# Turning the query maxima of a linear attention kernel: a transpose of 128 stationary columns in place of a product with 18

## The chip, the cores and the metric

The kernel runs on one core of a Trainium2 chip. The metric is the device time of one execution in microseconds (us). Three runs of the kernel before took 1091.09 to 1091.14 us, with a median of 1091.14.

## The reference, cut to what matters

A linear attention over 4 batches and 8 heads, 576 tokens of 64 numbers each, is followed by two feed-forward blocks. All inputs are float32.

```python
def phi(x):                                  # for q and for k
    proj = einsum('bhsd,df->bhsf', x, w_phi)            # 64 -> 128 features
    proj = proj - max(abs(proj), axis=-1)               # one maximum per token and head
    return concatenate([exp(proj), exp(-proj)], axis=-1)
kv, z = einsum('bhsf,bhsd->bhfd', phi(k), v), sum(phi(k), over s)
x = (phi(q) @ kv) / (phi(q) . z + 1e-6)                 # (2304, 512) in all
h = x @ moe_w_in;   x = maximum(0.01 * h, h) @ moe_w_out             # 512 -> 2048 -> 512
g = x @ moe2_w_gate
out = (g * sigmoid(g) * (x @ moe2_w_val)) @ moe2_w_out               # 512 -> 1536 -> 512
```

The change touches the line with the maximum, for the queries alone.

## The kernel before, in words

**Precision.** Most large products are made of parts: a float32 operand is split into a high and a low part of TensorE's float32r type (a copy on ScalarE and a subtraction on VectorE), and three products high*high, high*low and low*high are summed in PSUM. These are the rows with 128 x 288 outputs: a half of a batch, 288 tokens, is one PSUM bank. A plain float32 product takes two passes in the hardware, so it has two LDWEIGHTS and two MATMUL in the trace; a float32 transpose (`k_tr`, line 240) has one of each.

**Stages.** Attention of batch 0 comes first, alone. After that the feed-forward layers of batch b run as a list of "units" (`u_l1`, `u_gate`, `u_val`, `u_out`; the matmuls of line 615, for batch 3 and one block of batch 2 those of line 741), and the attention of batch b + 1 is spread between them: its keys beside the first block, its queries beside the second. So the queries of batches 1, 2 and 3 stand at about 187 to 340, 465 to 600 and 740 to 850 us of the span. The last batch has only feed-forward layers beside it.

**Queries.** For batches 1 to 3 the work of a batch is 8 groups: 4 pairs of heads (j), each in two halves of 288 tokens (t). For one group:

- `q_p` projects with features on the partitions (lines 336 and 337, two heads, one PSUM bank of 288 columns each), turns blocks of 32 x 32 on VectorE (338) and takes maxima (340). What is left is `m`, tile `mqt`: 128 partitions x 18. Partition 32 g + i, column (head, k) holds the maximum over the 32 features of block g for token 32 k + i.
- `q_m_t` turns `m` on TensorE, so that the 4 feature blocks lie in one partition: a matmul with `m` as the stationary operand (18 columns) and the identity as the moving one (line 346). The result goes into unused columns 288 to 415 of the group's second PSUM bank, partitions 0 to 17. VectorE then takes the maximum over the 4 blocks (348), splits it (351, 59) and lays it out as `mrow` with a 0/1 mask (356).
- `q_exp` adds minus the maximum to the projections by a matmul (367) and ScalarE makes the two exponentials (375, 376). `q_num` multiplies with the keys' sums (393), `q_fin` divides (401 to 411) and writes `xh` and `xl`, which the first layer reads.

In batch 1 the numerator (393) is a plain float32 product, in batches 2 and 3 it is made of float32r parts.

**Constants.** `cst_sb` is one SBUF tile of 128 partitions: the identity `ident` (128 columns), then `mask` (18) and `mask_t` (9). It is loaded once. `k_tr` reads `ident` as well.

**Order.** The program is written out as calls; the Tile framework then orders each engine's instructions by priorities and by a simulated time line (`schedule_with_timeline_sim=True`). The engines run their lists in order, and wait for each other by semaphores that the framework sets from the tiles' regions. All loads are issued on SyncE. So a changed cost of one instruction can change the order of others.

Of the kernel before, what the change touches and what calls it, by code (L numbers as in the profile page):

```python
# [7 lines left out]
F32 = mybir.dt.float32  # L8
# [9 lines left out]
P = 128  # L18
# [9 lines left out]
HT = S // 2  # L28

NB = HT // 32  # L30

NC = P + 18 + NB

OFF = (0, 128, 256, 352, 448)
VAL = (128, 128, 96, 96, 128)
# [6 lines left out]
def linear_attention_two_mlps(ctx: ExitStack, tc, qT, kT, vt, w_phi, w1, w2, wg, wv, w3, cst, out):  # L42
    nc = tc.nc
    act, dve, pe, pool = nc.scalar, nc.vector, nc.tensor, nc.gpsimd
# [9 lines left out]
    def T(shape, dt, tag, bufs, pool=sb):  # L54
        uid[0] += 1
        return pool.tile(shape, dt, tag=tag, name=f"{tag}_{uid[0]}", bufs=bufs)

    def sub(o, a, b):
        dve.tensor_tensor(out=o, in0=a, in1=b, op=ALU.subtract)  # L59
# [3 lines left out]


    cst_sb = const.tile([P, NC], F32, name="cst_sb")
    ident = cst_sb[:, 0:P]
    mask = cst_sb[:, P : P + 18]
    mask_t = cst_sb[:, P + 18 : NC]
    sel = const.tile([P, 4, P], F32R, name="sel")
    ones = const.tile([P, P], F32R, name="ones")  # L70
    wst_h = const.tile([P, F], F32R, name="wst_h")
# [6 lines left out]
    def constants():  # L78
        signs = T([P, 4, P], F32, "es", 5)
        nc.sync.dma_start(out=cst_sb, in_=cst[:, 0:NC])  # L80
        nc.sync.dma_start(out=signs.rearrange("p h f -> p (h f)"), in_=cst[:, NC:])
        zero = T([P, F], F32, "es", 5)
# [12 lines left out]
    def bk(b=1):  # L95

        if b == 0:
            return T([P, 512], F32, "pm", 4, psm)
        return T([P, 512], F32, "pa", 4, psa)
# [186 lines left out]
    qs, pt, mq, mrow, qfh, qfl, qn, dn = ({} for _ in range(8))  # L286
# [41 lines left out]
    def q_p(b, j, t):  # L328

        c = slice(HT * t, HT * t + HT)  # L330
        tp = T([P, 2, NB, 32], F32, "pk", 5)
        for h in range(2):
            bank = pt[b, j, h, t] = bk(b)
            ps = bank[:, 0:HT]
            a = qs[b, j][h][:, c]
            pe.matmul(ps, wst_h, a, start=True, stop=False)
            pe.matmul(ps, wst_l, a, start=False, stop=True)
            dve.transpose(out=tp[:, h].rearrange("p a b -> p (a b)"), in_=ps)
        m = mq[b, j, t] = T([P, 2, NB], F32, "mqt", 2)
        dve.tensor_reduce(out=m, in_=tp, axis=AX.X, op=ALU.max, apply_absolute_value=True)  # L340

    def q_m_t(b, j, t):

        m = mq.pop((b, j, t)).rearrange("p h k -> p (h k)")
        turned = pt[b, j, 1, t][0 : 2 * NB, HT : HT + P]
        pe.matmul(turned, m, ident, start=False, stop=True, skip_group_check=True)  # L346
        top = T([2 * NB, 32], F32, "top", 2)
        dve.tensor_reduce(out=top, in_=turned.rearrange("r (g i) -> r i g", g=4), axis=AX.X, op=ALU.max)
        x = mm[2 + t]
        hi = x[0 : 2 * NB]  # L350
        dve.tensor_copy(hi, top)
        sub(x[32 : 32 + 2 * NB], top, hi.bitcast(F32))
        if t == 0:
            mrow[b, j] = T([P, 2 * NB, 32], F32R, "mrow", 1)
        r = mrow[b, j][:, NB * t : NB * t + NB]
        dve.tensor_tensor(
            out=r,
            in0=x.bitcast(F32).rearrange("p (o i) -> p o i", o=1).to_broadcast([P, NB, 32]),
            in1=mask_t.rearrange("p (k o) -> p k o", o=1).to_broadcast([P, NB, 32]),
            op=ALU.mult,  # L360
        )
# [79 lines left out]
    def q_steps_t(b):  # L441


        groups = [(j, t) for j in range(NP) for t in range(2)]
        n = len(groups)
        steps = []
        for i in range(n + 2):
            one, two = [], []
            if i >= 2:
                j, t = groups[i - 2]  # L450
                one.append(lambda j=j, t=t: q_num(b, j, 0, t))
                two.append(lambda j=j, t=t: (q_num(b, j, 1, t), q_fin(b, j, t)))
            if 1 <= i <= n:
                j, t = groups[i - 1]
                one.append(lambda j=j, t=t: q_exp(b, j, 0, t))
                two.append(lambda j=j, t=t: q_exp(b, j, 1, t))
            if i < n:
                j, t = groups[i]
                if t == 0:
                    one.append(lambda j=j: q_split(b, j))  # L460
                one.append(lambda j=j, t=t: q_p(b, j, t))
                two.append(lambda j=j, t=t: q_m_t(b, j, t))
                if t == 1 and j + 1 < NP:
                    two.append(lambda j=j: load_q(b, j + 1))
                if t == 1 and j + 1 == NP and b + 1 < B:
                    two.append(lambda: load_k(b + 1, 0))
            steps += [one, two]
        return steps
# [586 lines left out]
    pre, made, start = 8, 0, 30  # L1055
# [26 lines left out]
def _constants():  # L1082
    import numpy as np

    c = np.zeros((P, NC + 4 * P), np.float32)
    c[:, 0:P] = np.eye(P)
    signs = c[:, NC:].reshape(P, 4, P)
    blocks = [(s, a) for s in range(NST) for a in range(VAL[s] // 32)]
    for p in range(P):
        a, r = divmod(p, 32)  # L1090
        if r >= 4 * NST:
            continue
        st, h = divmod(r % (2 * NST), 2)
        signs[p, h] = -1.0
        for k, (s2, a2) in enumerate(blocks):
            c[p, P + k] = float(s2 == st and a2 == a)
    for part in (0, 32):
        for h in range(2):
            for k in range(NB):
                c[part + NB * h + k, P + 18 + k] = 1.0  # L1100
                signs[part + NB * h + k, 2 + h] = -1.0
    return c

# [47 lines left out]
```

## Time and profile before

| | |
|---|---|
| three runs, median (lowest to highest) | 1091.14 us (1091.09 to 1091.14) |
| the profiled execution: its span, first to last instruction | 1092.6 us |
| TensorE matmul busy in it | 1062.8 us, 97% |
| VectorE, ScalarE, GpSimd busy | 808.8, 656.2, 21.8 us |
| mean granted TensorE clock | 0.997 of 2.4 GHz |
| line 346, matmuls (24 calls, two passes each) | x48, 9.4 us of busy time |

The page shows no time around the span of the profiled execution; that span is 1.5 us longer than the median of the timed runs. Busy time of TensorE is the union of matmuls that overlap in a pipeline: a 128 x 288 matmul is shown with 298 ns, but one starts every 0.13 us. What an instruction costs TensorE is therefore read from the distance of starts, not from its duration.

### The profile page before, as it was taken

The numbers are of one execution on the slowest core, as the hardware profiler recorded it, in microseconds if no ns is written. First come the engines' busy times: TensorE is split into PE (matmuls) and PEld (weight loads), VectorE is DVE, ScalarE is ACT, GpSimd is POOL, SyncE is SP. The second block draws the span as 40 slices with busy tenths as digits, with TensorE's granted clock in tenths as the row PEclk, the third lists the DMA queues.
The fourth block names the chain that finished last, engine by engine and source line by source line (L and its number), as shares of the span: only waits on it lengthen the run. The fifth ranks groups of instructions, "written<-read, shape, count | busy, mean of one in ns | idle before, by whom it ended". The sixth has DMA issues, their size and how long they took to land.

```text
span 1092.6 us, 20353 instructions
## 1 busy us (share of the span) xinstructions
PE 1062.8 (97%) x7560; PEld 1023.3 (94%) x7560; DVE 808.8 (74%) x1761; ACT 656.2 (60%) x1467; POOL 21.8 (2%) x56
## 2 busy tenths in 40 slices
PE   7889999999999999999999988999999999999998
PEld 6668999989899999999999988999999999999998
DVE  6897797888899888779676864857779742458473
ACT  7878886768777787546553575644542334426441
POOL 1000100000000000000000000000000000000000
PEclk9999999999999999999999998999999999999999
DMA  9736767555666887767454386346978768748652
GB/s 326 235 114 204 240 208 259 172 183 177 210 201 230 335 304 268 263 237 242 164 177 145 111 332 235 126 175 228 313 243 297 287 216 303 275 157 306 216 178 96
DMA packets 98771, 245.61 MB, mean 225 GB/s; under 512 B 19952, under 2 KB 28400, under 8 KB 98672
## 3 DMA queue, kind: packets, MB, share of 16 engines
q1 hardware_dynamic: 94640, 229.62, 60.6%
q0 software_dynamic: 4032, 14.68, 3.4%
q8 instruction: 60, 0.98, 0.4%
q14 instruction: 39, 0.32, 0.1%
HBM read 178.73 MB, written 65.54 MB: 224 GB/s over the span
## 4 chain that ended last, share of the span: by engine, by line
PE 80%; DMA 8%; ACT 6%; DVE 4%; issue 1%; SPq 1%; ACTq 0%; DVEq 0%
PE pm L615 55%; PE pa L741 8%; PE pm L741 4%; PE pa L202 4%; PE pa L393 3%; DMA wi<-in_w_dram 2%; DMA wi<-parts 2%; PE pa L161 2%; DMA wr<-kept 1%; ACT wr L519 1%; DMA sums<-wr 1%; DVE wr L534 1%; PE pm L301 1%; PE pa L346 1%; ACT wi L520 0%
## 5 line engine op out<-in xcount | busy, mean ns | idle before, releaser
L615 PE MATMUL pm<-xh,wi 128*128 128x288 f32 x1664 | 351.7, 298 | 2.4 <-DVE es L656 1.8
L615 PE MATMUL pm<-gp,wo 128*128 128x288 f32 x2256 | 337.5, 297 | 0.8 <-DVE acc L682 0.5
L615 PEld LDWEIGHTS pm<-gp,wo 128*128 128x128 f32 x2256 | 311.1, 188 | 5.2 <-issue 1.9
L615 PEld LDWEIGHTS pm<-xh,wi 128*128 128x128 f32 x1664 | 271.8, 188 | 6.8 <-DVE es L656 2.3
L615 PE MATMUL pm<-xl,wi 128*128 128x288 f32 x832 | 246.7, 297 | 0.0
L615 PEld LDWEIGHTS pm<-xl,wi 128*128 128x128 f32 x832 | 156.3, 188 | 1.4 <-issue 0.6
L682 DVE TENSOR_TENSOR acc<-pm,acc 128x288 f32<-128x288 f32 x160 | 70.5, 450 | 45.2 <-PE pm L615 43.1
L59 DVE TENSOR_TENSOR gp<-es,gp 128x576 fp32r<-128x576 f32 x94 | 70.5, 751 | 29.9 <-ACT gp L62 29.2
L62 ACT ACTIVATE gp<-es 128x576 fp32r<-128x576 f32 x94 | 64.3, 688 | 27.9 <-DVE es L663 22.8
L741 PE MATMUL pm<-xh,wi 128*128 128x288 f32 x304 | 71.6, 303 | 6.0 <-DMA wi<-parts 5.2
L59 DVE TENSOR_TENSOR wi<-wr,wi 128x512 fp32r<-128x512 f32 x96 | 64.8, 682 | 13.2 <-ACT wi L544 12.8
L544 ACT ACTIVATE wi<-wr 128x512 fp32r<-128x512 f32 x96 | 59.5, 633 | 13.1 <-PE pm L615 5.2
L741 PEld LDWEIGHTS pm<-xh,wi 128*128 128x128 f32 x304 | 53.2, 193 | 7.8 <-DVE fl L59 3.7
L59 DVE TENSOR_TENSOR fl<-ff,fh 128x512 fp32r<-128x512 f32 (+1 forms) x72 | 50.9, 712 | 11.0 <-ACT fh L62 10.8
L520 ACT ACTIVATE wi<-wi 128x512 int32<-128x512 uint32 x60 | 41.5, 692 | 23.1 <-DMA wi<-in_wv_dram 10.7
L519 ACT ACTIVATE wr<-wi 128x512 f32<-128x512 f32 x60 | 41.2, 690 | 16.4 <-DMA wi<-in_w_dram 8.6
L396 ACT ACTIVATE dn<-pa 64x288 f32<-64x288 f32 x64 | 26.0, 406 | 36.1 <-PE pa L393 35.2
L62 ACT ACTIVATE fh<-ff 128x512 fp32r<-128x512 f32 (+1 forms) x72 | 47.0, 664 | 0.8
L643 ACT ACTIVATE es<-pm 128x288 f32<-128x288 f32 x72 | 28.8, 418 | 29.7 <-PE pm L741 17.1
L741 PE MATMUL pm<-xl,wi 128*128 128x288 f32 x152 | 45.6, 300 | 0.0
L534 DVE TENSOR_TENSOR wr<-wr,wi 128x512 uint16<-128x512 uint16 x60 | 44.9, 751 | 0.8
L202 PE MATMUL pa<-ff,pk 128*128 128x256 f32 (+1 forms) x160 | 42.6, 383 | 2.4 <-issue 1.9
(192 smaller groups left out, 2073.4 us busy)
## 6 DMA issues: line engine op xcount, KB each, us to landing
wi<-parts SPq DMA_DIRECT2D x96, 512.0 KB, 5.9
wo<-parts SPq DMA_DIRECT2D x77, 512.0 KB, 6.6
parts<-wi SPq DMA_DIRECT2D x56, 512.0 KB, 4.6
wi<-in_w_dram SPq DMA_DIRECT2D x44, 512.0 KB, 5.1
wr<-kept SPq DMA_DIRECT2D x72, 256.0 KB, 4.2
parts<-wo POOLq DMA_DIRECT2D x28, 512.0 KB, 5.1
kept<-wr SPq DMA_DIRECT2D x40, 256.0 KB, 4.2
wi<-in_wv_dram SPq DMA_DIRECT2D x12, 512.0 KB, 4.1
```

The lines of the kernel that those rows point to most:

```text
L59: dve.tensor_tensor(out=o, in0=a, in1=b, op=ALU.subtract)
L62: act.activation(o, a, AF.Copy)
L202: pe.matmul(ps[:, 256 * h : 256 * h + 256], v[:n, h].rearrange("p a d -> p (a d)"), part[b, j, s][:n, h].rearrange("p a f -> p (a f)"), st ...
L393: pe.matmul(ps, w, x, start=(i == 0), stop=(i == len(ops) - 1))
L519: act.activation(t, high.bitcast(F32), AF.Abs, scale=REBIAS)
L520: act.activation(low, low.bitcast(U32), AF.Copy, scale=2.0**-29)
L534: dve.tensor_tensor(out=t16, in0=t16, in1=e16, op=ALU.add)
L544: i = act.activation(t[:, 0], r, AF.Copy)
L615: m = pe.matmul(ps, w, x[:, c], start=(i == 0), stop=(i == n - 1))
L643: act.activation(o, i, AF.Prelu, alpha=0.01)
L682: dve.tensor_tensor(out=acc[o][:, t], in0=ps, in1=acc[o][:, t], op=ALU.add)
L741: m = pe.matmul(ps, a, b, start=start and n == 0, stop=stop and n == 5, skip_group_check=True)
```

## The change

The maxima no longer go to a tile of their own. `cst_sb` grows by 36 columns in front of the identity. Two windows of 128 columns, `tops[0]` (columns 0 to 127) and `tops[1]` (18 to 145), begin with the 18 columns that the maxima of half t = 0 or t = 1 are written to. `q_m_t` gives the whole window to TensorE as stationary operand, in transpose mode, and writes 128 x 128 numbers to PSUM, of which partitions 0 to 17 are read as before. What stands in the other columns of a window (the other half's maxima, part of the identity) ends in partitions that nobody reads. The constants' load grows from 155 to 191 columns.

```diff
-NC = P + 18 + NB
+TOPS = 4 * NB
+NC = TOPS + P + 18 + NB
...
-    ident = cst_sb[:, 0:P]
-    mask = cst_sb[:, P : P + 18]
-    mask_t = cst_sb[:, P + 18 : NC]
+    tops = [cst_sb[:, 2 * NB * t : 2 * NB * t + P] for t in range(2)]
+    ident = cst_sb[:, TOPS : TOPS + P]
+    mask = cst_sb[:, TOPS + P : TOPS + P + 18]
+    mask_t = cst_sb[:, TOPS + P + 18 : NC]
...
-        m = mq[b, j, t] = T([P, 2, NB], F32, "mqt", 2)
+        m = tops[t][:, 0 : 2 * NB].rearrange("p (h k) -> p h k", h=2)
         dve.tensor_reduce(out=m, in_=tp, axis=AX.X, op=ALU.max, apply_absolute_value=True)

     def q_m_t(b, j, t):

-        m = mq.pop((b, j, t)).rearrange("p h k -> p (h k)")
-        turned = pt[b, j, 1, t][0 : 2 * NB, HT : HT + P]
-        pe.matmul(turned, m, ident, start=False, stop=True, skip_group_check=True)
+        turned = pt[b, j, 1, t][:, HT : HT + P]
+        pe.matmul(
+            turned, tops[t], ident, is_transpose=True, start=False, stop=True, skip_group_check=True
+        )
+        turned = turned[0 : 2 * NB]
         top = T([2 * NB, 32], F32, "top", 2)
```

The columns of `_constants` move by the same 36.

The order of instructions changes with it, in the stretches of the span in which batches 1 to 3 have their queries. On TensorE the kernel has the same matmuls in both, and 1340 of the 7315 in its list stand at another place, by at most 68 places; between 566 and 709 us of the span before, and from 813 us on, the orders agree.

VectorE, batch 3, first pair of heads, before. The second row is the maximum of half t = 0 (line 340), the sixth that of half t = 1, and the tenth the reduction behind the turn of half t = 0 (348); `pk` is the tile of turned blocks.

```order
L338 STREAM_TRANSPOSE pk_9791<-pa_9796 128x288
L340 TENSOR_REDUCE mqt_9660<-pk_9651 128x18
L682 TENSOR_TENSOR acc_8634<-pm_9611,acc_8634 128x288
L59 TENSOR_TENSOR pk_9960<-raw_9861,pk_9960 64x576
L682 TENSOR_TENSOR acc_8634<-pm_9625,acc_8634 128x288
L340 TENSOR_REDUCE mqt_9800<-pk_9791 128x18
L59 TENSOR_TENSOR pk_9961<-raw_9861,pk_9961 64x576
L682 TENSOR_TENSOR acc_8700<-pm_9662,acc_8700 128x288
L682 TENSOR_TENSOR acc_8700<-pm_9676,acc_8700 128x288
L348 TENSOR_REDUCE top_9697<-pa_9656 18x32
```

The same place now. Lines of the program are 1 to 4 higher in the changed kernel: 338 is 340, 340 is 342, 348 is 352, 59 is 60 and 682 is 686.

```order
L340 STREAM_TRANSPOSE pk_9774<-pa_9779 128x288
L342 TENSOR_REDUCE cst_sb<-pk_9635 128x18
L686 TENSOR_TENSOR acc_8618<-pm_9595,acc_8618 128x288
L60 TENSOR_TENSOR pk_9942<-raw_9843,pk_9942 64x576
L686 TENSOR_TENSOR acc_8618<-pm_9609,acc_8618 128x288
L60 TENSOR_TENSOR pk_9943<-raw_9843,pk_9943 64x576
L686 TENSOR_TENSOR acc_8684<-pm_9645,acc_8684 128x288
L686 TENSOR_TENSOR acc_8684<-pm_9659,acc_8684 128x288
L352 TENSOR_REDUCE top_9680<-pa_9640 18x32
L342 TENSOR_REDUCE cst_sb<-pk_9774 128x18
```

The maximum of half t = 1 stood ahead of the reduction `top` of half t = 0 and now stands behind it. In the other 23 groups it stands behind it in both kernels.

TensorE, batch 1, the turn of the last of the 8 groups, before (line 346; `gp` and `wo` are operands of the second layer, `xh`, `xl` and `wi` of a layer of the block behind it).

```order
L615 MATMUL pm_3893<-gp_3670,wo_3679 128x288 x3
L615 MATMUL pm_3893<-gp_3765,wo_3776 128x288
L615 MATMUL pm_3843<-gp_3765,wo_3776 128x288 x2
L615 MATMUL pm_3857<-gp_3765,wo_3776 128x288 x2
L615 MATMUL pm_3893<-gp_3765,wo_3776 128x288 x2
L346 MATMUL pa_3700<-cst_sb,mqt_3704 18x128
L615 MATMUL pm_3907<-gp_3422,wo_3433 128x288 x3
```

The same turn now (line 347; 619 is the former 615).

```order
L619 MATMUL pm_4027<-xh_2557,wi_3871 128x288
L619 MATMUL pm_4027<-xh_2606,wi_3871 128x288
L619 MATMUL pm_4027<-xl_2607,wi_3871 128x288
L347 MATMUL pa_3693<-cst_sb 128x128
L619 MATMUL pm_4027<-xh_2606,wi_3871 128x288
L619 MATMUL pm_4027<-xh_2651,wi_3871 128x288
L619 MATMUL pm_4027<-xl_2652,wi_3871 128x288
```

It has moved 68 matmuls later, from the output layer into the next unit. The last numerator of this group (393) moved 35 matmuls later, and the first matmul that reads this group's `xh` in the feed-forward layers of batch 1 stands at the same place of the list in both.

## Rows read from the trace of the kernel before

**Rows 1.** The page, its head and the busy time of engines.

```profile
span 1092.6 us, 20353 instructions
...
PE 1062.8 (97%) x7560; PEld 1023.3 (94%) x7560; DVE 808.8 (74%) x1761; ACT 656.2 (60%) x1467; POOL 21.8 (2%) x56
```

**Rows 2.** Stretches: length, busy PE, PEld, DVE, ACT, POOL; clock, DMA share, GB/s.

```profile
187.00:320.00 133.00, 130.20 (x910) 122.34 (x909) 117.19 (x247) 100.55 (x203) 5.84 (x11) 1.00 0.59 194
465.00:600.00 135.00, 135.00 (x1005) 132.00 (x1005) 102.30 (x224) 68.72 (x149) 0.00 (x0) 1.00 0.56 192
740.00:850.00 110.00, 109.39 (x809) 106.06 (x809) 90.94 (x222) 49.68 (x112) 0.00 (x0) 1.00 0.75 261
```

**Rows 3.** Line 346: durations in ns (min/median/max), first and last start.

```profile
L346 PEld LDWEIGHTS pa<-cst_sb,mqt x48: 93/96/98, 191.5 to 840.0; 128*18 128x18 f32 x48
L346 PE MATMUL pa<-cst_sb,mqt x48: 272/278/286, 191.5 to 840.1; 128*18 128x128 f32 x48
```

**Rows 4.** Time line of PE around the first turn: start, length in us, instruction.

```profile
191.15 0.42 PE L615 MATMUL pm<-xh,wi 128*128 128x288 f32 x2
191.50 0.39 PE L346 MATMUL pa<-cst_sb,mqt 128*18 128x128 f32 x2
191.83 0.40 PE L615 MATMUL pm<-xl,wi 128*128 128x288 f32 x1
192.06 0.42 PE L615 MATMUL pm<-xh,wi 128*128 128x288 f32 x2
```

**Rows 5.** Line 240, the transposes of the keys' sums.

```profile
L240 PEld LDWEIGHTS pa<-cst_sb,kvz x64: 138/140/146, 17.7 to 716.7; 128*128 128x128 f32 x64
L240 PE MATMUL pa<-cst_sb,kvz x64: 270/272/328, 17.7 to 716.8; 128*128 128x128 f32 x64
```

**Rows 6.** Time line of PE around single transposes of line 240.

```profile
180.86 0.96 PE L615 MATMUL pm<-gp,wo 128*128 128x288 f32 x6
181.66 0.27 PE L240 MATMUL pa<-cst_sb,kvz 128*128 128x128 f32 x1
181.68 0.38 PE L615 MATMUL pm<-gp,wo 128*128 128x288 f32 x1
181.90 0.27 PE L240 MATMUL pa<-cst_sb,kvz 128*128 128x128 f32 x1
```

**Rows 7.** The chain that ended last: its first and last turn (19 such).

```profile
220.14 0.32 PE pa L346 x2
...
840.00 0.34 PE pa L346 x2
```

**Rows 8.** The chain, longest pieces at 187 to 209, 284 to 309, 762 to 795 us.

```profile
188.70 3.75 DMA wi<-in_wv_dram
...
285.70 5.27 DMA wi<-in_w_dram
...
769.27 7.43 DMA sums<-wr
```

**Rows 9.** What PE waited for, 185 to 325 us: us, times, longest.

```profile
PE pm L615 <- DVE es L656: 1.7, 1, 1.7
```

**Rows 10.** Time line of VectorE, batch 3: maximum t = 1, `top` t = 0.

```profile
743.42 0.74 DVE L340 TENSOR_REDUCE mqt<-pk 128x18 f32<-128x576 f32 x1
...
745.71 0.27 DVE L348 TENSOR_REDUCE top<-pa 18x32 f32<-18x128 f32 x1
```

**Rows 11.** The last numerators (PE) and last results (VectorE, 318 to 345 us) of batch 1.

```profile
328.17 2.10 PE L393 MATMUL pa<-ff,kvh 128*128 128x288 f32 x8
...
L59 DVE TENSOR_TENSOR xl<-xf,xh x3: 444/446/452, 321.7 to 341.2; 128x288 fp32r<-128x288 f32 x3
```

**Rows 12.** PE's longest wait on its time line, and the stretches behind it.

```profile
677.77 0.58 PE L741 MATMUL pm<-xh,wi 128*128 128x288 f32 x1 [3.49 <-DMA wi<-parts]
...
677.00:683.80 6.80, 6.03 (x25) 5.96 (x26) 3.57 (x7) 1.85 (x4) 0.00 (x0) 0.50 0.73 288
684.00:690.00 6.00, 6.00 (x49) 5.96 (x48) 4.57 (x10) 5.15 (x11) 0.00 (x0) 1.00 0.28 89
```

More of the change, by code (lines that the diff above doesn't have):

```diff
@@ L1085, in _constants @@
     c = np.zeros((P, NC + 4 * P), np.float32)
-    c[:, 0:P] = np.eye(P)
+    c[:, TOPS : TOPS + P] = np.eye(P)
     signs = c[:, NC:].reshape(P, 4, P)
@@ L1095, in _constants @@
         for k, (s2, a2) in enumerate(blocks):
-            c[p, P + k] = float(s2 == st and a2 == a)
+            c[p, TOPS + P + k] = float(s2 == st and a2 == a)
     for part in (0, 32):
@@ L1099, in _constants @@
             for k in range(NB):
-                c[part + NB * h + k, P + 18 + k] = 1.0
+                c[part + NB * h + k, TOPS + P + 18 + k] = 1.0
                 signs[part + NB * h + k, 2 + h] = -1.0
```

## The prediction

> **What bounds the kernel now.** I read the page's busy times first, then the stretches in which the queries of batches 1 to 3 stand, then the chain that ended last, and last the time line of TensorE around the instructions in question. TensorE has matmuls running for 1062.8 of 1092.6 us [rows 1]. In the three stretches of the queries that is 130.2 of 133, 135.0 of 135 and 109.4 of 110 us; VectorE, the next busiest, has 117, 102 and 91 [rows 2]. So a slot saved on TensorE there is time saved, as long as nothing else stands just behind it. The chain shows where something does: of the 24 turns 19 lie on it (from the one at 220.14 to the one at 840.00 us [rows 7]), with five of batch 1, all eight of batch 2 and six of batch 3. The five others, at 191.5, 202.9, 290.4, 763.3 and 780.0 us, stand where the chain runs through VectorE, ScalarE and loads, whose longest pieces are the transfers of 3.75, 5.27 and 7.43 us [rows 8].
>
> **The price of a turn before.** A turn is one call and two passes: 24 calls give 48 matmuls of 278 ns [rows 3]. Those durations overlap with neighbours, so I take starts. From 191.15 to 192.06 us TensorE starts two rows of L615, the two passes, and one L615 more; the next L615 starts at 192.06 [rows 4]. That is 0.91 us for three ordinary matmuls and one turn. An ordinary one takes 0.133 us: six from 180.86 to 181.66, 0.80 us [rows 6]. So the turn costs 0.91 - 0.40 = 0.51 us.
>
> **The price of a turn after.** The trace has the very form already: the transposes of line 240 are float32, 128 x 128 stationary, 128 columns out, one LDWEIGHTS and one MATMUL each, 64 of them [rows 5]. At 181.66 and 181.90 us such transposes stand singly between ordinary matmuls: 0.24 us for one transpose and one L615 [rows 6], so 0.24 - 0.13 = 0.11 us for the transpose. What differs from line 240 is that the new call accumulates (start=False), into columns of a bank in which a projection already stands. No row shows that with transpose mode. Bounds: 0.11 us if it is like line 240, and 0.51 us if the hardware handles it as it handled the old call. I take 0.11, since the form and the number of instructions are those of line 240.
>
> Saved per turn: 0.51 - 0.11 = 0.40 us. Over 24 turns 9.6 us of TensorE's time, over the 19 on the chain 7.6 us.
>
> A place where a rule speaks against this. The weight load of the old call lasts 96 ns for 18 columns, that of line 240 140 ns for 128 [rows 3, 5]; the trace thus shows a longer load, though far from seven times as long. The Trainium skill (TensorE: Matmul & The Clock Gate, section LDWEIGHTS) says that the time of a load follows its columns, about columns / 1.2 in ns, which by its figures would be 15 ns and 107 ns. By the rule alone a turn that shows both loads would go from 2 x 15 to 107 ns; the rows have a fixed part that the rule lacks.
>
> In the rows the longer load is hidden: 0.11 us for a whole transpose is less than its load of 0.14 us, so the load runs beside the matmul ahead [rows 5, 6]. It can run ahead only if the maxima are there in time. If VectorE delivers them just as TensorE arrives, the load is bare and the turn costs 0.11 + 0.14 = 0.25 us: 0.26 saved, 4.9 us over 19 turns. That is a bound on the cautious side and goes into the range.
>
> **The other edits.** The maxima go to `cst_sb` in place of `mqt`: the same instruction on VectorE, no cost. The constants' load grows by 36 columns at the program's start, ahead of 17.7 us, when line 240 first reads it [rows 5]: nothing. PSUM gets 128 partitions in place of 18 in a stretch of the bank that nobody else uses: nothing that I can see.
>
> One wait is added. `tops[0]` covers columns 0 to 127, the columns 18 to 35 that the maxima of half t = 1 are written to among them. So the maximum of t = 1 has to wait until the turn of t = 0 has read its weights. In 23 of 24 groups the maximum stood behind the reduction `top` of the half before, which waits for the same turn anyway. In the first pair of batch 3 it didn't: it ran at 743.42 us and `top` at 745.71 [rows 10]. There the order now puts it behind `top`, 2.3 to 2.6 us later, and the turn that it feeds moves 21 matmuls later. Queued behind it on VectorE are sums out of PSUM (`acc`) and splits. They don't wait longer, since the order was changed instead of a wait being left in front of them. The exponentials of this group move by 5 to 8 matmuls, about 1 us. I put it at 0, with 1 us as its bound on the bad side.
>
> **What the order does.** The scheduler has moved 1340 of 7315 matmuls, by at most 68. [...] Of the distances between a turn and the exponential behind it the shortest is still 29 matmuls. The waits of TensorE in the moved part of batch 1 are led by one of 1.7 us [rows 9]; a new order draws them anew, as likely better as worse. I put this at 0 with 1.7 us to the good and 3.5 us, the longest wait in the trace [rows 12], to the bad.
>
> **The sum.** 1092.6 - 7.6 = 1085.0 us for the profiled execution. The runs' median is 1.5 us below its span, and a saving in TensorE's slots is the same for both: 1091.14 - 7.6 = 1083.5 us.
>
> **Rivals.**
>
> *Less comes through.* In batch 1 VectorE is busy for 117 of 133 us [rows 2] and the chain changes engines often, so the five turns there and the two at 742 and 746 us may only lengthen waits. Then 12 turns count: 12 x 0.40 = 4.8 us, 1086.3; with bare loads on 19 turns 1086.2; with one new wait of 3.5 us 1089.8. For it speaks the share of VectorE in batch 1; against it that batch 2 has no idle TensorE at all and a VectorE with a quarter of its time free [rows 2].
>
> *All of it, and a wait goes too.* 24 x 0.40 + 1.7 = 11.3 us, 1079.8. Against it: a chain of loads around 763 to 795 us that TensorE doesn't drive [rows 8].
>
> *Nothing changes.* The accumulating transpose is handled in two passes or takes as long as the old turn, 0.51 us: 1091. Against it: one MATMUL per transpose in rows 5.
>
> *Slower: the last group of batch 1 comes late.* Its turn stands 68 matmuls later, its last numerator 35 matmuls or 4.7 us later, while its first reader has kept its place in the list. Before, the numerators end at about 329.9 and the last `xl` is written at 341.2 + 0.45 = 341.7 us [rows 11]; the reader of that half stands 143 matmuls behind the last numerator in the order, at 329.9 + 143 x 0.133 = 348.9. The slack was 7.2 us and is now 2.5. The stretch from the numerators to `xl`, 11.8 us, holds mostly other work of a full VectorE queue. If it grows by more than 2.5 us, TensorE waits. The one wait of 3.49 us in the trace was followed by 6.8 us at a granted clock of 0.50, the lower of the two levels, 1.2 GHz, in which 25 matmuls took 6.03 us, while the 49 behind them took 6.00 [rows 12]: 3 us lost on top. So from a wait of 4.6 us on (4.6 + 3.0) the whole gain is gone. At 8 us it is 8 + 3 - 7.6 = 3.4 us slower: 1094.5. Against it: it takes a chain 7 us longer than the 11.8 us of today, with no work added to VectorE or ScalarE.
>
> *Slower: the clock.* Each turn as a transpose might bring TensorE to its lower level. If every one cost the 3 us of the case above, 24 would cost 72 us: 1156 with the gain taken off. Against it: the stretch at 465 to 600 us has a granted clock of 1.00 [rows 2], and transposes of line 240 stand between 17.7 and 716.8 us [rows 5], four of them single ones at 182 us, with ordinary matmuls at full pace right behind [rows 6].
>
> The Trainium skill (TensorE: Matmul & The Clock Gate, Part 4, PE-mode transpose) is the reason why I name this one: it says that the full clock does not engage in transpose mode, as the array doesn't count it as busy in the same way, and gives about 275 ns for a transpose in a kernel. The duration agrees with the 272 ns of rows 5; of the clock the rows show nothing here, because each transpose is alone among ordinary matmuls. By its 275 ns as the cost of a slot the gain would be 19 x (0.51 - 0.275) = 4.5 us, 1086.7.
>
> **Chances.** Forecast, 1081.5 to 1086: 0.60. Less comes through, 1086 to 1089: 0.17. More, under 1081.5: 0.08. Nothing changes, or the gain is eaten by waits: 0.07. Late group, about 1094.5: 0.07. Clock: 0.01. A measurement of this kernel tells a change from none at about 0.2%, 2.2 us. Faster than 1089.0 is thus 0.60 + 0.17 + 0.08 = 0.85, the same 0.07, slower 0.08. The range runs from all turns and the wait of 1.7 us gone, 1079.8, to 12 turns and one new wait of 3.5 us, 1089.8; I round it to 1079.5 and 1090.
>
> **What would show it.** In the profile after, line 347 has x24 in both rows, with a load of about 140 ns and a matmul of about 272. The matmul behind it starts 0.03 us after it, as behind line 240 [rows 6], not 0.33 us after the first pass [rows 4]. TensorE's busy time falls by about 9 us with the same clock. The turns of batch 2 bring 3.2 us between two matmuls that both kernels have in the same place, ahead of 471 and behind 576 us. From 600 us to 709, where the order is the same, both traces run in parallel, the wait of 3.49 us included. Wrong would be: starts of 0.3 us or more around line 347, a wait in front of it, a wait for `xl` in the first layer of batch 1, or a clock below 1.00 in the queries' stretches.

## The result, and the profile after

The changed kernel took 1083.57 us (median of 6 runs, 1082.31 to 1084.31). The kernel before took 1091.81 us (6 runs: the three at 1091.09 to 1091.14 that the forecast started from, and three more at 1092.47 to 1093.78). The ratio of runs taken next to each other is 0.9907 [0.9889, 0.9925], which is 10.2 us [8.2, 12.1] of 1091.81; the two medians are 8.2 us apart. A second series, with 17 runs of before, gave 1082.54 against 1092.27 us, 0.9913 [0.9897, 0.9928], 9.5 us [7.9, 11.3]. So the time came out as forecast (1083.5), and the gain somewhat above the 7.6 us of the sum.

The page after: the span, and each engine's busy time, share and instructions. TensorE has 24 matmuls fewer and is busy for 10.3 us less than in [rows 1].

```profile
span 1080.5 us, 20303 instructions
PE 1052.5 (97%) x7536; PEld 1021.8 (95%) x7536; DVE 809.5 (75%) x1761; ACT 655.4 (61%) x1467; POOL 21.6 (2%) x56
```

The stretches that answer to [rows 2], columns as there. TensorE is about as full as before at the same granted clock; the weight loads (PEld) now fill batches 2 and 3 too.

```profile
187.00:320.00 133.00, 129.12 (x920) 124.50 (x919) 118.77 (x249) 101.86 (x207) 5.85 (x11) 1.00 0.60 198
465.00:600.00 135.00, 134.58 (x1017) 134.34 (x1017) 104.65 (x232) 68.07 (x148) 0.00 (x0) 1.00 0.54 186
740.00:850.00 110.00, 110.00 (x833) 110.00 (x833) 94.83 (x233) 50.87 (x116) 0.00 (x0) 1.00 0.76 267
```

The instructions of the new line 347 by form (count, shortest/median/longest in ns, first and last start), where [rows 3] had 48 of each:

```profile
L347 PEld LDWEIGHTS pa<-cst_sb x24: 138/141/143, 190.2 to 828.3; 128*128 128x128 f32 x24
L347 PE MATMUL pa<-cst_sb x24: 270/272/304, 190.4 to 828.5; 128*128 128x128 f32 x24
```

The first turn on TensorE's time line, as in [rows 4]. The next matmul starts 0.03 us behind the turn, and the one after that 0.22 us later: 0.52 us from 190.09 to 190.61 for three ordinary matmuls and a turn, 0.12 of it the turn's.

```profile
190.09 0.43 PE L619 MATMUL pm<-xh,wi 128*128 128x288 f32 x2
190.36 0.27 PE L347 MATMUL pa<-cst_sb 128*128 128x128 f32 x1
190.39 0.38 PE L619 MATMUL pm<-xl,wi 128*128 128x288 f32 x1
190.61 0.42 PE L619 MATMUL pm<-xh,wi 128*128 128x288 f32 x2
```

**Where the time went.** For every kernel I numbered TensorE's matmuls in the order in which they start, the turns left out, and took the time between the starts of the same numbers: 1000 to 2000 covers the queries of batch 1, 3000 to 4000 those of batch 2, 4800 to 5750 those of batch 3. Two profiles of each of the two kernels (us):

```
matmuls        before  before again   after  after again   mean change
0-1000         182.73     181.73     181.61    180.49        -1.18
1000-2000      149.04     148.79     146.66    146.86        -2.16
2000-3000      131.14     131.28     130.99    130.99        -0.22
3000-4000      136.71     136.71     134.09    134.09        -2.62
4000-4800      117.25     114.14     115.06    116.02        -0.16
4800-5750      131.96     133.07     128.09    127.94        -4.50
5750-7511      235.67     235.79     235.84    236.55        +0.47
```

The three stretches of the queries bring 9.3 us; the sum had 2.0, 3.2 and 2.4, thus 7.6. The rest scatters: 4000 to 4800, in the same order in all, differs by 3.1 us between two executions of the kernel before.

A turn's slot, from start to start less the ordinary 0.133 us each, was 0.52 us before (typically 0.225, 0.121, 0.203 and 0.239 us around it) and is 0.11 now (0.133, 0.027, 0.217): 0.41 us each, 3.3 us for eight. Batch 1 got 2.2 of it; TensorE's waits there grew by 1.0 us. These are its waits after at 187 to 340 us (us, times, longest):

```profile
PE pm L619 <- DVE es L660: 1.7, 1, 1.7
PE pa L338 <- ACT ff L380: 1.2, 1, 1.2
PE pm L619 <- ACT wi L548: 0.8, 1, 0.8
```

Before, beside the 1.7 us of [rows 9], it had these in the same stretch (2.7 us in all):

```profile
PE pa L393 <- DVE xf L411: 0.5, 1, 0.5
PE pm L615 <- ACT gp L62: 0.3, 1, 0.3
PE pm L615 <- DVE wi L59: 0.2, 1, 0.2
```

Batch 2 got 2.6, since one wait came up where there had been none. On TensorE's time line it costs 0.58 us, 0.715 from the start before instead of 0.133:

```profile
486.00 0.29 PE L339 MATMUL pa<-pk,wst_l 128*128 128x288 f32 x1
486.72 0.40 PE L619 MATMUL pm<-xh,wi 128*128 128x288 f32 x1 [0.42 <-DVE es L660]
```

Batch 3 got more than its turns. The two longest waits of the kernel before at 720 to 850 us:

```profile
PE pm L615 <- ACT es L643: 0.6, 1, 0.6
PE pa L346 <- DVE mqt L340: 0.4, 1, 0.4
```

The longest of the kernel before in its second profile:

```profile
PE pa L346 <- DVE mqt L340: 1.5, 1, 1.5
```

The only one after; no wait stands at line 347:

```profile
PE pm L619 <- DMA wo<-parts: 0.7, 1, 0.7
```

So a turn of batch 3 had itself waited for its maxima, 0.4 us in one execution and 1.5 in the other, and doesn't any more: 3.3 + 0.4 and 3.3 + 1.5 make most of the 3.9 and 5.1 us. That the wait went belongs to the order, and not to the new call: in other kernels with the maxima in `cst_sb` a turn of batch 3 still waits for them (e1 0.2, e2 0.9, e6 0.7 us; e4 has none).

### The profile page after: what moved, and what is told of

It is laid out like the page before. It is cut to its first block, busy times and chain, and to the rows that moved or that the text cites. A ratio compares the mean times of both kernels' runs of the same rounds, so it can differ in the third digit from the quotient of the medians.

```text
span 1080.5 us, 20303 instructions
## 1 busy us (share of the span) xinstructions
PE 1052.5 (97%) x7536; PEld 1021.8 (95%) x7536; DVE 809.5 (75%) x1761; ACT 655.4 (61%) x1467; POOL 21.6 (2%) x56
## 4 chain that ended last, share of the span: by engine, by line
PE 82%; DMA 7%; ACT 5%; DVE 3%; issue 1%; SPq 0%; POOL 0%; ACTq 0%; DVEq 0%; POOLq 0%
PE pm L619 56%; PE pa L745 9%; PE pm L745 4%; PE pa L204 4%; PE pa L397 4%; DMA wi<-in_w_dram 3%; PE pa L163 2%; DMA wi<-parts 2%; DMA wi<-in_wv_dram 2%; ACT wr L523 1%; DVE wr L538 1%; PE pm L303 1%; PE pa L242 1%; PE pm L163 1%; PE pa L338 1%
```

## The experiments

All are counted in the same way, in us. A turn's slot is the median of its 24 turns. "Old" and "new" are the orders of before and after on TensorE, VectorE and ScalarE; "old*" differs from old in 22 places, and "own" is neither. In e3 and e4 some turns have the old slot and some the new.

```
run            slot    batch 1, order   batch 2, order   batch 3, order
before         0.52    149.04  old      136.71  old      131.96  old
before again   0.52    148.79  old      136.71  old      133.07  old
after          0.11    146.66  new      134.09  new      128.09  new
after again    0.11    146.86  new      134.09  new      127.94  new
e1             0.11    146.56  new      134.05  new      128.96  own
e2             0.22    149.19  old      134.31  old      130.11  own
e3             both    147.53  own      136.66  old      133.71  own
e4             both    147.87  own      134.08  new      128.94  own
e6             0.22    149.48  old*     134.29  old      129.36  as e2
e7             0.74    147.94  own      138.34  own      132.38  own
e8             0.11    147.66  new      190.10  own      127.66  new
```

**e1: transpose mode with 18 columns.** The mode alone, with the weights as narrow as before.

```diff
-        turned = pt[b, j, 1, t][:, HT : HT + P]
+        turned = pt[b, j, 1, t][0 : 2 * NB, HT : HT + P]
-            turned, tops[t], ident, is_transpose=True, ...
+            turned, tops[t][:, 0 : 2 * NB], ident, is_transpose=True, ...
```

> The turn in transpose mode, but with the 18 columns of the maxima alone as stationary operand (out to 18 partitions). Theory 1 (what the old turn cost is its two passes and the change to a plain float32 product and back): one pass in transpose mode is enough, whatever the columns; 0.11 us a turn, as the changed kernel: 24 x 0.41 = 9.8 us faster than before. Rival (the full 128 columns are what makes the weights' load run beside the matmul ahead): about 0.2 to 0.25 us a turn, 6.5 to 7.5 us faster.

Measured: 1085.44 us (1081.92 to 1086.87), 0.9935 [0.991, 0.996]; a turn's slot is 0.11 us. On TensorE's time line:

```profile
191.15 0.43 PE L619 MATMUL pm<-xh,wi 128*128 128x288 f32 x2
191.42 0.27 PE L347 MATMUL pa<-cst_sb 128*18 128x128 f32 x1
191.44 0.38 PE L619 MATMUL pm<-xl,wi 128*128 128x288 f32 x1
191.66 0.42 PE L619 MATMUL pm<-xh,wi 128*128 128x288 f32 x2
```

In transpose mode the 128 columns are not needed for the short slot. Batches 1 and 2 have the order of after and its times. The whole was 7.1 us [4.4, 9.8] faster than before, less than the 9.8 of theory 1; batch 3 has an order of its own and took 0.9 us longer than after.

**e2: 128 columns without transpose mode.** The width alone, with two passes as before.

```diff
-            turned, tops[t], ident, is_transpose=True, start=False, ...
+            turned, tops[t], ident, start=False, ...
```

> The turn with the 128 stationary columns, but as a plain float32 product in two passes. Theory 1: the two passes and the change of product stay, and each of two loads grows from 0.096 to 0.14 us: 0.51 to 0.60 us a turn, so 0 to 2.2 us slower than before. Rival (the 18 columns, a part of the array, were the costly thing): a turn of 0.25 us or less, 6 us or more faster than before.

Measured: 1088.3 us (1085.38 to 1090.49), 0.9958 [0.9942, 0.9973]. That is 4.6 us [2.9, 6.3] faster, where the rival had 6 or more. The two passes cost 0.22 us, 0.30 less than with 18 columns; 24 of these are 7.2 us, and not all of it came through. TensorE's time line:

```profile
190.76 0.42 PE L619 MATMUL pm<-xh,wi 128*128 128x288 f32 x2
191.02 0.38 PE L347 MATMUL pa<-cst_sb 128*128 128x128 f32 x2
191.16 0.38 PE L619 MATMUL pm<-xl,wi 128*128 128x288 f32 x1
191.38 0.43 PE L619 MATMUL pm<-xh,wi 128*128 128x288 f32 x2
```

Its weight loads there follow one another without a gap:

```profile
190.62 0.32 PEld L619 LDWEIGHTS pm<-xh,wi 128*128 128x128 f32 x2
190.89 0.32 PEld L347 LDWEIGHTS pa<-cst_sb 128*128 128x128 f32 x2
191.13 0.19 PEld L619 LDWEIGHTS pm<-xl,wi 128*128 128x128 f32 x1
```

Those of the kernel before stop twice around the turn of [rows 4], for 0.16 and 0.21 us; these loads start within 0.01 us of their matmuls, which start at 191.50 and 191.83 in [rows 4]:

```profile
191.50 0.12 PEld L346 LDWEIGHTS pa<-cst_sb,mqt 128*18 128x18 f32 x2 [0.16 <-issue]
191.82 0.19 PEld L615 LDWEIGHTS pm<-xl,wi 128*128 128x128 f32 x1 [0.21 <-issue]
```

So the old 0.52 us was 2 x 0.11 of passes and 0.30 of loads that didn't run ahead. Either half of the change ends the 0.30, and transpose mode takes one pass off as well. The change between kinds of product, which theory 1 blamed, is in e2 too and costs nothing there. Nor is it the tile that the maxima come from: the plain turns of 18 columns in e3 and e4 read them out of `cst_sb` and cost 0.52 us as well.

This kernel also tells what the order does. But for a few early swaps its instructions stand in the same order as before's on TensorE, VectorE and ScalarE through batches 1 and 2. In batch 2 the eight turns bring 8 x 0.30 = 2.40 us to the last digit (136.71 to 134.31). In batch 1 the same 2.4 us bring nothing: 149.19 against 149.04 and 148.79. Of the 1.8 us that six turns had saved by 275 us TensorE was 0.67 us ahead, and it lost that again at 284 to 286 us, where the chain runs through the load at 285.70 us [rows 8]. In e2 that load starts at the same time of the span, 285.74 us:

```profile
284.92 0.77 DVE wr L538
285.74 4.96 DMA wi<-in_w_dram
```

**e3 and e4: the change for five turns, and for the other nineteen.** The five are those that the chain didn't name.

```diff
+        if (b, 2 * j + t) in ((1, 0), (1, 1), (1, 6), (3, 2), (3, 3)):   # e4: not in
             (transpose of tops[t], as after)
+        else:
+            turned = pt[b, j, 1, t][0 : 2 * NB, HT : HT + P]
+            m = tops[t][:, 0 : 2 * NB]
+            pe.matmul(turned, m, ident, start=False, stop=True, ...)
```

> Only the five turns that did not lie on the chain of before (1st, 2nd and 7th of batch 1, 3rd and 4th of batch 3) are made in transpose mode; the other 19 are plain products of 18 columns, out of the same columns of the constants' tile. Theory A (every slot saved on TensorE counts, wherever the chain runs): 5 x 0.41 = 2.0 us faster than before. Theory B (only turns on the chain count, as predicted): 0 us, same as before. Waits drawn anew by another order may shift either by 1 to 2 us.

> The other 19 turns in transpose mode, the five plain. Theory A: 19 x 0.41 = 7.8 us faster than before, 2.0 us short of the changed kernel. Theory B: 7.8 us faster, and as fast as the changed kernel is.

Measured: the five 1092.93 us (1088.37 to 1095.03), 1.0002 [0.9987, 1.0018]; the nineteen 1085.7 us (1083.56 to 1088.02), 0.994 [0.9918, 0.9962], 6.6 us. The 0 of the five looks like the chain's word, but the stretches say otherwise. The five brought 1.3 to 1.5 us in batch 1 (147.53) and lost 0.6 to 1.7 in batch 3 (133.71), by the two profiles of before; another 1.2 was lost at 2000 to 3000, where no turn stands and the order is its own. The loss in batch 3 is waits. Three of e3's five at 715 to 855 us, two of them waits of turns for maxima which now go to `cst_sb`:

```profile
PE pa L376 <- DVE mrow L365: 1.0, 1, 1.0
PE pa L355 <- DVE cst_sb L342: 0.8, 1, 0.8
PE pa L348 <- DVE cst_sb L342: 0.5, 1, 0.5
```

Each subset gets an order of its own. So the 0 of the five doesn't show that these turns are worth nothing. The nineteen show the contrary: e4 is 2 to 3 us short of the changed kernel, as theory A had it, and that where its five plain turns stand. Batch 3, with two of them, took 0.9 us longer than after (2 x 0.41 = 0.8), batch 1, with three, 1.1 (3 x 0.41 = 1.2), batch 2, with none, the same. Batches 1 and 3 have orders of their own, so this is a sum that agrees, and not a proof for each turn.

**e5: the changed kernel once more**, in the series beside the others.

> The changed kernel again, timed beside the kernel before on one chip, since the two sets of runs of before differ (1091.1 and 1092.5 to 1093.8 us). Theory A (all 24 slots count): 9.8 us faster. Theory B (19 count): 7.6 to 7.8 us faster.

Measured: 1082.54 us (1080.93 to 1084.16), given above; 9.5 us is the firmer figure of the two, since all runs of before belong to one series.

**e6 and e7: the turn doubled, new and old.** Each turn is issued a second time into columns that nobody reads.

```diff
+        spare = pt[b, j, 0, t][:, HT : HT + P]          # e7: [0 : 2 * NB, ...] of before
+        pe.matmul(spare, tops[t], ident, is_transpose=True, ...)   # e7: the old call with m
```

> The changed kernel with each turn issued twice, the second into unused columns of the group's first bank. A transpose among ordinary matmuls costs 0.11 us: 24 x 0.11 = 2.6 us slower than the changed kernel, 7 us faster than before. Rival (a transpose costs its duration of 0.27 us): 6.5 us slower than the changed kernel.

> The kernel before with each turn issued twice, the second into unused columns of the group's first bank. Theory 1 (part of the old cost is the change between kinds of product, paid once for a row of plain products): the second call adds two passes of about 0.12 us, 24 x 0.24 = 5.8 us slower than before. Rival (each plain call costs 0.51 us): 12.2 us slower. Theory B of the chain would take a fifth off either.

Measured: e6 1086.69 us (1085.36 to 1088.62), 0.9952 [0.9937, 0.9966], 4.1 us above after. e7 1093.0 us (1091.69 to 1094.21), 1.0007 [0.9997, 1.0018]. The second transpose costs 0.11 us, as the first did, on e6's time line:

```profile
469.87 0.27 PE L347 MATMUL pa<-cst_sb 128*128 128x128 f32 x1
469.98 0.27 PE L351 MATMUL pa<-cst_sb 128*128 128x128 f32 x1
470.00 0.77 PE L623 MATMUL pm<-gp,wo 128*128 128x288 f32 x4
```

The second old call starts 0.23 us after the first, and the turn's slot goes from 0.52 only to 0.74. Loads of e7 there:

```profile
191.65 0.11 PEld L346 LDWEIGHTS pa<-cst_sb,mqt 128*18 128x18 f32 x2 [0.16 <-issue]
191.77 0.21 PEld L348 LDWEIGHTS pa<-cst_sb,mqt 128*18 128x18 f32 x2
192.19 0.19 PEld L617 LDWEIGHTS pm<-xl,wi 128*128 128x128 f32 x1 [0.21 <-issue]
```

No load stops between the two calls; the stops are at the way in and the way out. So the 0.30 us is paid once for a visit and each pass adds 0.11. Batch 2 bears it out: 138.34 us, 1.63 above before, where 8 x 0.216 is 1.73. The whole moved by 0.8 us [-0.3, 2.0] and not by 24 x 0.216 = 5.2: in orders of their own batch 1 was 0.9 to 1.1 us shorter than before, with eight dearer turns, and batch 3 lay between the two profiles of before. So a new order can give back as much as dearer turns cost.

That e6 is 4.1 us above after, and not the 2.6 expected, isn't the transposes' price either. Its order is e2's but for 22 places in batch 1, and there it took 149.48 us, as before and e2 did, 2.7 more than after; 8 x 0.11 is 0.9. In the profiled execution the clock has a part in it: behind a wait of 2.0 us for `es` the granted clock was 0.50, the level of 1.2 GHz, from 227.6 to 231.0 us.

**e8: 64 more transposes behind each turn of batch 2**, for the clock.

```diff
+        for _ in range(64 if b == 2 else 0):
+            pe.matmul(spare, tops[t], ident, is_transpose=True, ...)
```

> The changed kernel with 64 more transposes behind each turn of batch 2, into unused columns: 8 stretches of nothing but transposes. If transposes keep TensorE at its granted clock of 1.00: 64 x 0.109 = 7.0 us a turn, 56 us in all, clock 1.00 throughout batch 2's queries. If in transposes alone the clock falls to 0.50: each stretch has part of its rows at 0.50 and is longer, up to 14 us a turn, 112 us in all.

Measured: 1139.9 us, one run. Batch 2 took 190.10 us, 56.0 more than after; 8 x 64 x 0.109 is 55.8. Its window has the clock at 1.00:

```profile
465.00:655.00 190.00, 190.00 (x1522) 190.00 (x1521) 108.26 (x227) 70.58 (x148) 0.00 (x0) 1.00 0.39 133
```

The eight stretches of nothing but transposes that were expected didn't come: the scheduler set ordinary matmuls between. Most transposes stand one by one, but some in rows, five of them of 16 to 50. The longest on the time line is the turn and 49 more, 5.4 us at a clock of 1.00:

```profile
531.15 0.27 PE L347 MATMUL pa<-cst_sb 128*128 128x128 f32 x1
531.26 5.51 PE L352 MATMUL pa<-cst_sb 128*128 128x128 f32 x49
536.53 0.38 PE L624 MATMUL pm<-xh,wi 128*128 128x288 f32 x1
```

**e9: the kernel before once more**, for what one profile is worth.

> The kernel before again, for a second profile. If the lengths of the stretches of the queries belong to the order of instructions, they come out as in the first profile: batch 1 (common matmuls 1000 to 2000) 149.0 us, batch 2 (3000 to 4000) 136.7, batch 3 (4800 to 5750) 132.0, each within 0.3 us, while the stretch of loads at 600 to 715 us (4000 to 4800) and the start scatter by 1 to 3 us. If they don't, what the orders seem to be worth is chance.

Measured: 1091.5 us, one run; its stretches stand in the table above. Batches 1 and 2 came out within 0.25 us, so their changes of 2.2 and 2.6 us are the kernel's. Batch 3 was 1.1 us longer, more than the 0.3 expected, by the wait for `mqt`.

## Why the prediction was right, and which term was off

**The price per turn: right.** Forecast 0.51 - 0.11 = 0.40 us, measured 0.52 - 0.11 = 0.41. The accumulating transpose is like that of line 240, the load is hidden, and the rival "nothing changes" is out. What the prediction couldn't tell is what the 0.51 us was made of: e2 and e7 show 0.22 of passes and 0.30 for a visit.

The Trainium skill (TensorE: Matmul & The Clock Gate, section LDWEIGHTS), by which the time of a load follows its columns, would have made the narrow load the cheaper one. As a duration it is, 96 ns of [rows 3] against 188 in e2 for the same plain product; but the turn with the narrow one took 0.52 us and that with the wide one 0.22. What counted was whether the load ran ahead.

**"19 turns on the chain": the mis-sized term.** It gave 2.0, 3.2 and 2.4 us; measured were 2.2, 2.6 and 4.5. That the time was hit within 0.1 us is in part luck: the gain was 1.9 to 2.6 us larger than the sum, and the runs of before beside it were 0.7 to 1.1 us longer than the 1091.14 that it was taken from.

- In batch 3 six turns were counted, and all eight came through: the stretch has one wait left (0.7 us) and TensorE is full. The two at 763 and 780 us, put down as beside the chain because it runs through a transfer there [rows 8], gave their slots all the same: where e4 left them plain, batch 3 was 0.9 us longer. Besides, the wait of a turn for `mqt` went.
- In batch 2 all eight counted, as forecast, less the new wait of 0.6 us, which had been put at 0. It comes with the new order: after, its second profile, e1 and e4 have it (0.4 us in their lists of waits), e2 and e6 in the old order have none.
- In batch 1 the size is right (2.0 against 2.2), but not for the reason given, five slots on the chain; that is luck. At the old order e2 turned 2.4 us of saved slots into nothing, so something else than TensorE sets the pace there (the chain names loads, ScalarE and VectorE), as the rival "less comes through" had it. What batch 1 gained came with the new order: four executions of it took 146.56 to 147.66 us, four of the old one, e6's 22 places aside, 148.79 to 149.48, with slots of 0.52 or 0.22 us. So it isn't chance. The 147.66 is e8's, with a clock of 0.50 from 210.6 to 214.0 us.

So "what the order does", put at 0, was about +2 us in batch 1, +0.4 to +1.5 in batch 3 and -0.6 in batch 2, and it is not a cost of the change that could be read from the trace of before. e3's loss in batch 3 shows that such an order can as well take it back.

**The added wait: right, as far as can be seen.** In the first pair of batch 3 the maximum of t = 1 runs directly behind `top` of t = 0, where [rows 10] had it 2.3 us ahead. VectorE's time line after:

```profile
736.78 0.27 DVE L352 TENSOR_REDUCE top<-pa 18x32 f32<-18x128 f32 x1
736.98 0.73 DVE L342 TENSOR_REDUCE cst_sb<-pk 128x18 f32<-128x576 f32 x1
```

Its turn, at 740.1 us, had nothing to wait for. The matmul behind the turn before, at 733.66, started 0.31 us late, since its weight load waited for a sum (`acc`) on VectorE:

```profile
734.00 0.43 PEld L619 LDWEIGHTS pm<-gp,wo 128*128 128x128 f32 x3 [0.23 <-DVE acc L686]
```

e1 has the same, although its narrow operands don't overlap and its maximum of t = 1 stands ahead of `top` as before (734.94 and 737.24 us):

```profile
733.80 0.43 PEld L619 LDWEIGHTS pm<-gp,wo 128*128 128x128 f32 x3 [0.27 <-DVE acc L686]
```

So these 0.31 us are not the price of the added wait, of which nothing is seen.

**The late group of batch 1: not come.** No matmul of batch 1's first layer waits for `xl`. The last three are written as early as in [rows 11], whose numerators end at 330.3 us and not at the 329.9 of the prediction, which doesn't touch its slack:

```profile
L60 DVE TENSOR_TENSOR xl<-xf,xh x3: 451/453/453, 322.1 to 341.3; 128x288 fp32r<-128x288 f32 x3
```

**The clock: not come.** It is 1.00 in the three stretches. The Trainium skill (TensorE: Matmul & The Clock Gate, Part 4, PE-mode transpose) says that the full clock doesn't engage in transpose mode. e8, with 512 more transposes in 190 us at 1.00, in rows of up to 50, doesn't bear that out; nothing but transposes for longer than 5.4 us was not tried. The Trainium skill's 275 ns agrees with a transpose's duration (272) and not with its slot (0.11 us).

**"From 600 us to 709 both run in parallel": wrong.** The order is the same, and yet that stretch (4000 to 4800) took from 114.0 us (e1) to 117.4 (e6), and two executions of before were 3.1 us apart. The wait of 3.49 us in [rows 12] was 2.72 after, and in the second profile of before it was another engine's:

```profile
676.35 0.37 PE L741 MATMUL pm<-xh,wi 128*128 128x288 f32 x1 [2.57 <-DVE fl L59]
```

The clock differed as well. Where the first profile of before had 6.8 us at 0.50 [rows 12], after had 3.4:

```profile
671.80:675.20 3.40, 3.40 (x17) 3.30 (x16) 1.84 (x4) 1.69 (x3) 0.00 (x0) 0.50 0.99 374
```

The second profile of before had none; around its wait:

```profile
674.00:684.00 10.00, 7.66 (x58) 7.55 (x59) 7.77 (x15) 8.02 (x18) 0.00 (x0) 1.00 0.84 315
```

So of the 12.1 us between the two spans some 3 us, at the start and here, are chance. The prediction's "1.5 us below its span" has the same source: a run's time is 1.7 to 1.9 us above its span wherever both are on record (1082.31 and 1080.5 for the profile after), so the first profile of before was an execution of about 1094.4 us, as an estimate, and not a typical one.

**What stays open.** Why the loads stop at 18 columns in a plain float32 product and not in transpose mode, and from which width on they don't: no run has a width between 18 and 128. Also how much of batch 1's gain an unchanged order would keep with the full 0.41 us: the old order was run with slots of 0.22 us (e2, e6), not with 0.11. Nor was the new order run with the old call.

## What to carry to other kernels

Take the cost of an instruction from the starts around it and look at the weight loads' own line: a stop there ("issue") before and behind a small product is a price that neither duration shows, and a wider operand or transpose mode ended it here. The chain of the old execution tells which slots TensorE could give back in the old order; where a scheduler draws the order anew, count every slot in a stretch that TensorE fills, and leave some 2 us to either side for the order, which is what it moved single stretches by here. Take the profile of the kernel before twice: a stretch in which two executions differ by 3 us can't be read for one.

## What the runs showed of the hardware that was not expected

A plain float32 product with 18 stationary columns among products with 128 cost 0.30 us for a visit beyond its passes, whether one or two stood together (before, e7). In transpose mode with 18 columns (e1) and in plain float32 with 128 (e2) that cost is gone. A pass with 128 moving columns costs 0.11 us from start to start in each of these forms, at a median duration of 271 to 279 ns, and in a row of 50 transposes too (e8). That row, of 5.4 us, ran at a granted clock of 1.00.
